# One planned order for every engine's queue is replaced by another: attention and a gated FFT convolution on one core

## The chip, the core and the metric

The kernel runs on one NeuronCore of a Trainium2 chip. The metric is the device time of one execution in microseconds (us). Before the change three runs gave 368.68, 367.60 and 368.24 us; their median is 368.24 us.

## What is computed

Eight batches go through attention with 12 heads of width 64 over 448 positions, whose softmax has an extra `exp(-m)` in the denominator. The heads are put side by side into 768 columns, and a gated convolution follows.

```python
scores = scale * np.matmul(q, k.transpose(0, 1, 3, 2))
m = np.max(scores, axis=-1, keepdims=True)
e = np.exp(scores - m)
attn = e / (np.sum(e, axis=-1, keepdims=True) + np.exp(-m) + 1e-09)
x = heads_side_by_side(np.matmul(attn, v))        # 8 x 448 x 768
proj = x @ w_proj                                 # 768 -> 3 * 768
x1, x2, x3 = the three thirds of proj
x2_conv = irfft(rfft(x2) * rfft(filter))          # along the 448 positions
out = (x1 * x2_conv * x3) @ w_out
```

## The kernel before

**Tiling.** Two heads make a pair; a batch `b` has six pairs, and the pairs of all batches are numbered `i` from 0 to 47. For a pair the kernel turns k and q so that the head width lies on the partitions (`T`, on TensorE and back by VectorE, for batches 0 and 1; `kT` and `qT`, by DMA transposes of three pairs at a time, from batch 2 on). Then come the scores `S(i, t)` (line 871, 873). `S(i, 0)` is one matmul of the full 128 rows, since the rests of both heads lie in it. `S(i, 1)` to `S(i, 3)` are *score couples*: two matmuls of 64 rows each, one for either head, which run side by side. ScalarE takes the exponentials (lines 884, 890). The product with v is `ER(i)` (eight small matmuls of 64 rows, line 902) and `V(i, 0)`, `V(i, 1)` (12 matmuls of 128 rows each, line 910). VectorE divides (lines 923 to 925) into `xb`.

From `xb` each batch gets its transposed `xT`: batch 0 on TensorE (`X`), the others by two DMA transposes of three pairs each (`X9` stands below for the one that carries pairs 9 to 11; line 977). The dense part of a batch follows: a fold on VectorE, the projection of x2 (`P` for batches 0 and 1, line 1083; `PS(b, 0)` to `PS(b, 5)` from batch 2 on, line 1105, with a DMA transpose `x2(b, 0)` or `x2(b, 1)` after each three, line 1122), the spectrum `Z` (lines 1154, 1158), the product with the filter's spectrum, the inverse `I` (line 1253), the two gates `G` (line 1206; `G4` is the first part of one whose sum over the six tiles is cut in two), and the output product `O` and `O4` (line 1019).

**Where data come from.** SyncE (SP) issues the loads of k, q and v (written `sk`, `sq`, `sv`, and `rk`, `rv` for the remaining 64 rows of all pairs of a batch), the DMA transposes and the stores, in one queue. GpSimd (POOL) casts the loaded tiles to bf16 (`ck`, `cq`, `cv`, `crk`, `crv`) and issues the loads of the weights in the same queue: `w(0)` for the first gate, `w(1,0)` and `w(1,1)` for the projection of x2, `w(2)` for the second gate (line 849), and `wout`.

**What sets the order.** No queue is written out by hand in the source. The kernel lists 2135 steps by `plan.add(engine, cost, want, emit, need, make, ...)`, then `plan.run` plays them through a small model of the core: at each moment an engine takes its next step if that step's needs are made and its room in PSUM and SBUF is free. A tuple `plan.ORDER` with one number for each step fixes the order within each engine: an engine's steps are sorted by their numbers.

```python
want = self.ORDER[len(self.tasks)] if self.ORDER else want + self.SHIFT.get(part, 0.0)
...
cost, dma, run, late = self.TIMES.get(len(self.tasks), (cost, dma, run, late))
...
queue = {e: sorted(t for t in self.tasks if t[2] == e) for e in self.LAT}
...
for i, t in enumerate(queue[e][: 1 if self.ORDER else self.WINDOW]):
```

So with ORDER given the model moves no step within an engine. It still decides which PSUM bank each step gets, and how many dummy matmuls on a zero tile (*fillers*, line 1501) stand on TensorE where the model sees it idle between 4.6 and 44 us (`FILL`, 90% of the idle time at 0.056 us each from 8 us on, `COLD` before). `plan.TIMES` holds the model's numbers for each transfer (issue cost, duration, length of run, lateness), and LANDING, DELAY, EARLY and TURN_ROOM are constants of the same model. The chip itself waits only for the data and the room that a step needs.

Of the kernel before, what the change touches and what calls it, by code (L numbers as in the profile page):

```python
# [1612 lines left out]
```

## Time and profile before

| | |
|---|---|
| runs shown | 367.60, 368.24, 368.68 us (median 368.24) |
| profiled execution, first to last instruction (its span) | 365.4 us |
| TensorE busy | 358.2 us, 98% of the span |
| VectorE, ScalarE, GpSimd busy | 261.7, 263.4, 114.0 us |
| DMA packets | 135299, 69.20 MB |
| granted TensorE clock | 1.000 |

No time of its own is shown for the profiled execution beyond its span; the median of the runs lies 2.84 us above that span, which is what lies around it (launch and end). In the profile PE is TensorE's matmuls and PEld its weight loads; a timeline row gives the start, the length, the engine, the line, the operation, what is written and read, and how many alike follow one another. Matmuls overlap in the pipe, so the length of one (0.35 us) says less than the distance from one start to the next.

### The profile page before, as it was taken

The numbers are of one execution on the slowest core, as the hardware profiler recorded it, in microseconds if no ns is written. First come the engines' busy times: TensorE is split into PE (matmuls) and PEld (weight loads), VectorE is DVE, ScalarE is ACT, GpSimd is POOL, SyncE is SP. The second block draws the span as 40 slices with busy tenths as digits, with TensorE's granted clock in tenths as the row PEclk, the third lists the DMA queues.
The fourth block names the chain that finished last, engine by engine and source line by source line (L and its number), as shares of the span: only waits on it lengthen the run. The fifth ranks groups of instructions, "written<-read, shape, count | busy, mean of one in ns | idle before, by whom it ended". The sixth has DMA issues, their size and how long they took to land. (4 is left out here: it accounts for less than half of the span.)

```text
span 365.4 us, 9379 instructions
## 1 busy us (share of the span) xinstructions
PE 358.2 (98%) x3628; PEld 213.2 (58%) x3629; DVE 261.7 (72%) x671; ACT 263.4 (72%) x453; POOL 114.0 (31%) x247
## 2 busy tenths in 40 slices
PE   7999999999999999999999999999999999999995
PEld 6777665656664555655565555654555556555653
DVE  5669299877899549785777758893677867759570
ACT  6989777778796668875777667888877885465433
POOL 7872363315333454345324442700110000000000
PEclk9999999999999999999999999999999999999999
DMA  8999989999999999999999999999942165035025
GB/s 204 270 253 240 248 170 230 230 207 216 157 251 268 249 225 247 200 268 229 260 215 224 309 206 210 210 226 189 219 108 43 45 88 131 0 88 130 26 110 175
DMA packets 135299, 69.20 MB, mean 189 GB/s; under 512 B 91917, under 2 KB 131664, under 8 KB 135248
## 3 DMA queue, kind: packets, MB, share of 16 engines
q1 hardware_dynamic: 130528, 62.90, 78.4%
q0 software_dynamic: 4480, 5.41, 8.8%
q8 instruction: 29, 0.48, 0.6%
q10 hardware_dynamic: 240, 0.23, 0.2%
q14 instruction: 22, 0.18, 0.2%
HBM read 43.86 MB, written 11.01 MB: 150 GB/s over the span
## 5 line engine op out<-in xcount | busy, mean ns | idle before, releaser
L884 ACT ACTIVATE e<-psum 128x896 bf16<-128x896 f32 x138 | 123.0, 922 | 28.8 <-PE psum L871 23.7
L1206 PE MATMUL psum<-xT,wproj_bf 128*128 128x448 bf16 x576 | 121.7, 352 | 0.2 <-DMA xT<-xb 0.2
L1206 PEld LDWEIGHTS <-wproj_bf 128*128 128x128 bf16 x576 | 53.9, 98 | 46.6 <-issue 3.4
L1019 PE MATMUL psum<-wout_bf,yT 128*128 128x384 bf16 (+2 forms) x287 | 54.1, 326 | 0.2
L1105 PE MATMUL psum<-xf,wproj_bf 128*128 128x456 bf16 x216 | 45.7, 356 | 0.0
L910 PE MATMUL psum<-vn,e 128*128 128x65 bf16 x1104 | 45.1, 194 | 0.0
L910 PEld LDWEIGHTS <-e 128*128 128x128 bf16 x1104 | 39.8, 98 | 8.9 <-issue 4.5
L871 PE MATMUL psum<-qT,kT 64*128 64x448 bf16 x288 | 41.9, 354 | 0.2 <-DMA kT<-nat 0.2
L1172 DVE TENSOR_TENSOR t<-xs,hrs 113x768 bf16<-113x768 bf16 (+1 forms) x64 | 39.1, 631 | 3.0 <-ACT xs L1166 2.8
L1222 DVE TENSOR_TENSOR g<-x,psum 128x448 bf16<-128x448 bf16 x42 | 26.0, 618 | 19.0 <-PE psum L1206 16.2
L1332 ACT COPY osb<-psum 128x384 f32<-128x384 f32 (+2 forms) x56 | 26.0, 485 | 17.7 <-PE psum L1019 13.1
L668 POOL CAST nat<-nat 112x512 bf16<-112x512 f32 x36 | 24.3, 679 | 44.1 <-DMA nat<-in_q_dram 44.1
L1166 ACT CAST xs<-psum 113x384 bf16<-113x384 f32 (+1 forms) x64 | 29.1, 484 | 12.3 <-PE psum L1154 8.4
L1019 PEld LDWEIGHTS <-yT 128*128 128x128 bf16 x288 | 27.1, 98 | 18.5 <-issue 1.2
L925 DVE TENSOR_TENSOR xb<-psum,den 128x512 bf16<-128x512 f32 x48 | 33.2, 691 | 1.7
L1220 ACT CAST x<-psum 128x448 bf16<-128x448 f32 x42 | 22.4, 539 | 13.3 <-PE psum L1206 11.7
L700 POOL CAST vn<-nat 128x192 bf16<-128x192 f32 x58 | 21.7, 406 | 32.9 <-DMA nat<-in_v_dram 31.0
L1262 ACT CAST cr<-psum 128x452 bf16<-128x452 f32 x48 | 24.5, 544 | 10.1 <-PE psum L1253 9.2
L1105 PEld LDWEIGHTS <-wproj_bf 128*128 128x128 bf16 x216 | 20.1, 98 | 19.7 <-issue 2.4
L890 ACT ACTIVATE er<-psum 128x448 bf16<-128x448 f32 x46 | 25.4, 555 | 6.9 <-PE psum L873 6.2
L688 POOL CAST nat<-nat 128x384 bf16<-128x384 f32 x29 | 17.6, 612 | 26.6 <-DMA nat<-in_k_dram 24.7
L923 DVE TENSOR_SCALAR den<-psum 128x8 f32<-128x8 f32 x48 | 7.9, 164 | 23.9 <-PE psum L910 23.3
(138 smaller groups left out, 482.0 us busy)
## 6 DMA issues: line engine op xcount, KB each, us to landing
...
```

The source lines that it names most:

```text
L871: nc.tensor.matmul(sc[:, u, 0:S], kT[b % 2][c, hp, t, :], qT[b % 2][c, hp, :])
L884: nc.scalar.activation(to, of, AF.Exp, scale=SCALE)
L890: nc.scalar.activation(to, of, AF.Exp, scale=SCALE)
L910: nc.tensor.matmul(out_bank(u)[:, n, :], P["e"][1 + t][:, u * S + n * 128 : u * S + n * 128 + 128], vn[b % 2][:, hp, 4 * u + t, :], start= ...
L925: nc.vector.tensor_tensor(W["xb", b][:, hp].rearrange("p n (u d) -> p u n d", u=2), op[:, :, :, 0:DH], rec[:].unsqueeze(3).to_broadcast([1 ...
L1019: nc.tensor.matmul(ops[:n, : c.stop - c.start], y[:, dt, 0:n], wout_bf[:, dt, c], start=(dt == 0), stop=(dt == NDT - 1),)
L1105: nc.tensor.matmul(pps, wproj_bf[:, kt, D + dt * 128 : D + (dt + 1) * 128], W["xf", b][:, kt], start=(kt == 0), stop=(kt == NDT - 1),)
L1166: nc.scalar.copy(L["xs", par, ch][:K, pg % 2, :], L["Z", pg, ch][:K, :DCH])
L1172: nc.vector.tensor_tensor(t[:K], L["xs", par, ch][:K], h, op=ALU.mult)
L1206: nc.tensor.matmul(p[:, :S], wproj_bf[:, kt, 2 * part * D + dt * 128 : 2 * part * D + (dt + 1) * 128], xT()[:, kt, 0:S], start=(kt == 0), ...
L1222: nc.vector.tensor_tensor(g[:, dt, :], L["x1", dt], p[:, :S], op=ALU.mult)
L1332: (nc.vector.tensor_copy if half else nc.scalar.copy)(L["os", st][:n, c.start + lo : c.start + hi], L["O", st, ch][:n, lo:hi])
```

## The change

Only constants and the two tables of the plan are changed. Every step, its operands and its needs stay as they were.

```diff
-    LANDING = 1.738
-    DELAY = (0.917, 3.66)
-    EARLY = ((3.0, -0.67), (13.0, 0.95))
-    TURN_ROOM = 1.05
+    LANDING = 1.23
+    DELAY = (1.42, 2.33)
+    EARLY = ((0.0, 0.0), (0.0, 0.0))
+    TURN_ROOM = 1.2
...
-    plan.ORDER = (3, 0, 1, 124, 1, 2, 0, 0, 1, 2, 3, 4, 2, 4, 18, 0, 1, 5, 0, 7, ...
-    plan.TIMES = {3: (0.64, 0.05, 256.0, 0.0), 15: (0.58, 0.735, 50.0, 0.104), 16: (0.58, 1.17, 50.0, -0.215), ...
+    plan.ORDER = (1, 0, 3, 144, 2, 3, 0, 0, 4, 1, 2, 3, 4, 1, 27, 0, 4, 5, 0, 4, ...
+    plan.TIMES = {3: (0.64, 0.0456, 305.26, 0.2144), 15: (0.52, 0.7518, 83.32, 0), 16: (0.52, 0.6399, 70.62, 0), ...
```

In TIMES the old table has a lateness of its own for each transfer (between -4.3 and 4.6 us); the new one has one duration and one lateness for each kind of transfer (0 for the loads, between -0.32 and 0.21 us for the others).

Sorting each engine's steps by the two ORDER tuples gives the queues. 590 of PE's 712 steps change place, by 3.7 places on average and 33 at most; SP 218 of 246, ACT 378 of 451, DVE 481 of 548, POOL 153 of 178. What the prediction speaks of:

| queue | before | after |
|---|---|---|
| PE, first steps | spin, bps, T0, T(0) of k, T(0) of q, S(0,0), S(0,1), S(0,2), T(1) | spin, T(0) of q, T(0) of k, S(0,1), S(0,2), S(0,3), bps, T0, T(1), S(0,0) |
| ACT, first steps | sq0, zero ks, sine table, sines, exp table, exponentials of pair 0 | sq0, sine table, sines, exp table, zero ks, exponentials of pair 0 |
| SP, first loads | sk0, rk0, sk1, sq1, sq2, sk2, sv0, sq3 | sk0, rv0, sq1, sk1, rk0, sq2, sk3, sk2 |
| POOL around `w(0)` | ..., cq5, cv3, `w(0)`, crk1, crk1, `w(1,0)`, cq6 | ..., cq5, `w(0)`, cv3, crk1, cv4, crk1, ones, cq6, cq7, cv5, ck7, `w(1,0)` |
| POOL around `w(2)` | cv7, ck10, `w(2)`, wout, cq11 | cv7, cv9, cv10, cq11, `w(2)`, ck10, wout |
| PE: place of the first step that reads `w(0)` | 74 | 72 |
| PE: place of the first step that reads `w(2)` | 129 (second gate, tile 1) | 128 (second gate, tile 0) |
| PE: runs of steps of 64 rows in all / from the first step that reads `w(0)` / from the first that reads `w(2)` | 82 / 66 / 58 | 77 / 64 / 56 |
| longest run (steps) | 3 | 4 |
| PE between the last of PS(2,3..5) and the first Z that reads x2(2,1) | 3 G, 4 V, 4 couples, S(21,0), ER, 2 Z, in 2 runs | 3 G, 2 V, 2 couples, S(21,0), ER, 2 Z, in 1 run |
| PE between the last of PS(4,0..2) and the first Z that reads x2(4,0) | 2 PS, 3 V, 3 couples, S(33,0), 2 ER, 2 G | 2 PS, 4 V, 3 couples, S(33,0), S(34,0), 2 ER |
| PE between the last V of batch 4 and the first G of batch 4 | 3 G, 5 I, 2 O, 2 couples, S(31,0), S(30,0) | 4 G, 5 I, O, O4, 2 couples, S(30,0) |
| PE between the last G of batch 7 and the first closing O of it | O4, O4, O4 | O4, O4 |

A run is a stretch of PE steps of 64 rows (score couples and ER) with no step of more rows between.

More of the change, by code (lines that the diff above doesn't have):

```diff
@@ new lines @@
+    plan.TIMES = {3: (0.64, 0.0456, 305.26, 0.2144), 15: (0.52, 0.7518, 83.32, 0), 16: (0.52, 0.6399, 70.62, 0), 18: (0.52, 0.9263, 103.83, 0), 20: (0.52, 0.7518, 83.32, 0), 21: (0.52, 0.6399, 70.62, 0), 32: (0.52, 0.7518, 83.32, 0), 34: (0.52, 0.9263, 103.83, 0), 36: (0.52, 0.7518, 83.32, 0), 41: (0.52, 0.7518, 83.32, 0), 43: (0.52, 0.9263, 103.83, 0), 45: (0.52, 0.7518, 83.32, 0), 50: (0.52, 0.7518, 83.32, 0), 52: (0.52, 0.9263, 103.83, 0), 54: (0.52, 0.7518, 83.32, 0), 59: (0.52, 0.7518, 83.32, 0), 61: (0.52, 0.9263, 103.83, 0), 63: (0.52, 0.7518, 83.32, 0), 68: (0.52, 0.7518, 83.32, 0), 70: (0.52, 0.9263, 103.83, 0), 72: (0.52, 0.7518, 83.32, 0), 77: (0.52, 0.7518, 83.32, 0), 78: (0.52, 0.6399, 70.62, 0), 80: (0.52, 0.9263, 103.83, 0), 82: (0.52, 0.7518, 83.32, 0), 83: (0.52, 0.6399, 70.62, 0), 91: (0.52, 0.7518, 83.32, 0), 93: (0.52, 0.9263, 103.83, 0), 95: (0.52, 0.7518, 83.32, 0), 100: (0.52, 0.7518, 83.32, 0), 102: (0.52, 0.9263, 103.83, 0), 104: (0.52, 0.7518, 83.32, 0), 109: (0.52, 0.7518, 83.32, 0), 111: (0.52, 0.9263, 103.83, 0), 113: (0.52, 0.7518, 83.32, 0), 118: (0.52, 0.7518, 83.32, 0), 120: (0.52, 0.9263, 103.83, 0), 122: (0.52, 0.7518, 83.32, 0), 127: (0.52, 0.7518, 83.32, 0), 129: (0.52, 0.9263, 103.83, 0), 131: (0.52, 0.7518, 83.32, 0), 136: (0.52, 0.6399, 70.62, 0), 137: (0.52, 0.6399, 70.62, 0), 141: (0.52, 0.9263, 103.83, 0), 143: (1.29, 0.9672, 8.99, -0.3239), 144: (0.52, 0.7518, 83.32, 0), 146: (1.29, 0.7211, 18, -0.3239), 147: (0.52, 0.7518, 83.32, 0), 149: (0.52, 0.9263, 103.83, 0), 151: (1.29, 0.9672, 8.99, -0.3239), 152: (0.52, 0.7518, 83.32, 0), 154: (1.29, 0.7211, 18, -0.3239), 155: (0.52, 0.7518, 83.32, 0), 157: (0.52, 0.9263, 103.83, 0), 159: (1.29, 0.9672, 8.99, -0.3239), 160: (0.52, 0.7518, 83.32, 0), 162: (1.29, 0.7211, 18, -0.3239), 163: (0.52, 0.7518, 83.32, 0), 165: (0.52, 0.9263, 103.83, 0), 167: (1.29, 0.9672, 8.99, -0.3239), 168: (0.52, 0.7518, 83.32, 0), 170: (1.29, 0.7211, 18, -0.3239), 171: (0.52, 0.7518, 83.32, 0), 173: (0.52, 0.9263, 103.83, 0), 175: (1.29, 0.9672, 8.99, -0.3239), 176: (0.52, 0.7518, 83.32, 0), 178: (1.29, 0.7211, 18, -0.3239), 179: (0.52, 0.7518, 83.32, 0), 181: (0.52, 0.9263, 103.83, 0), 183: (1.29, 0.9672, 8.99, -0.3239), 184: (0.52, 0.7518, 83.32, 0), 186: (1.29, 0.7211, 18, -0.3239), 187: (0.52, 0.7518, 83.32, 0), 189: (0.52, 0.6399, 70.62, 0), 190: (0.52, 0.6399, 70.62, 0), 194: (0.52, 0.9263, 103.83, 0), 196: (1.53, 1.6028, 18, -0.3239), 197: (0.52, 0.7518, 83.32, 0), 199: (1.53, 1.8351, 18, -0.3239), 200: (0.52, 0.7518, 83.32, 0), 202: (0.52, 0.9263, 103.83, 0), 204: (0.52, 0.7518, 83.32, 0), 206: (0.52, 0.7518, 83.32, 0), 208: (0.52, 0.9263, 103.83, 0), 210: (0.52, 0.7518, 83.32, 0), 212: (0.52, 0.7518, 83.32, 0), 214: (0.52, 0.9263, 103.83, 0), 216: (1.53, 1.6028, 18, -0.3239), 217: (0.52, 0.7518, 83.32, 0), 219: (1.53, 1.8351, 18, -0.3239), 220: (0.52, 0.7518, 83.32, 0), 222: (0.52, 0.9263, 103.83, 0), 224: (0.52, 0.7518, 83.32, 0), 226: (0.52, 0.7518, 83.32, 0), 228: (0.52, 0.9263, 103.83, 0), 230: (0.52, 0.7518, 83.32, 0), 232: (0.52, 0.7518, 83.32, 0), 234: (0.52, 0.6399, 70.62, 0), 235: (0.52, 0.6399, 70.62, 0), 239: (0.52, 0.9263, 103.83, 0), 241: (1.53, 1.6028, 18, -0.3239), 242: (0.52, 0.7518, 83.32, 0), 244: (1.53, 1.8351, 18, -0.3239), 245: (0.52, 0.7518, 83.32, 0), 247: (0.52, 0.9263, 103.83, 0), 249: (0.52, 0.7518, 83.32, 0), 251: (0.52, 0.7518, 83.32, 0), 253: (0.52, 0.9263, 103.83, 0), 255: (0.52, 0.7518, 83.32, 0), 257: (0.52, 0.7518, 83.32, 0), 259: (0.52, 0.9263, 103.83, 0), 261: (1.53, 1.6028, 18, -0.3239), 262: (0.52, 0.7518, 83.32, 0), 264: (1.53, 1.8351, 18, -0.3239), 265: (0.52, 0.7518, 83.32, 0), 267: (0.52, 0.9263, 103.83, 0), 269: (0.52, 0.7518, 83.32, 0), 271: (0.52, 0.7518, 83.32, 0), 273: (0.52, 0.9263, 103.83, 0), 275: (0.52, 0.7518, 83.32, 0), 277: (0.52, 0.7518, 83.32, 0), 279: (0.52, 0.6399, 70.62, 0), 280: (0.52, 0.6399, 70.62, 0), 284: (0.52, 0.9263, 103.83, 0), 286: (1.53, 1.6028, 18, -0.3239), 287: (0.52, 0.7518, 83.32, 0), 289: (1.53, 1.8351, 18, -0.3239), 290: (0.52, 0.7518, 83.32, 0), 292: (0.52, 0.9263, 103.83, 0), 294: (0.52, 0.7518, 83.32, 0), 296: (0.52, 0.7518, 83.32, 0), 298: (0.52, 0.9263, 103.83, 0), 300: (0.52, 0.7518, 83.32, 0), 302: (0.52, 0.7518, 83.32, 0), 304: (0.52, 0.9263, 103.83, 0), 306: (1.53, 1.6028, 18, -0.3239), 307: (0.52, 0.7518, 83.32, 0), 309: (1.53, 1.8351, 18, -0.3239), 310: (0.52, 0.7518, 83.32, 0), 312: (0.52, 0.9263, 103.83, 0), 314: (0.52, 0.7518, 83.32, 0), 316: (0.52, 0.7518, 83.32, 0), 318: (0.52, 0.9263, 103.83, 0), 320: (0.52, 0.7518, 83.32, 0), 322: (0.52, 0.7518, 83.32, 0), 324: (0.52, 0.6399, 70.62, 0), 325: (0.52, 0.6399, 70.62, 0), 329: (0.52, 0.9263, 103.83, 0), 331: (1.53, 1.6028, 18, -0.3239), 332: (0.52, 0.7518, 83.32, 0), 334: (1.53, 1.8351, 18, -0.3239), 335: (0.52, 0.7518, 83.32, 0), 337: (0.52, 0.9263, 103.83, 0), 339: (0.52, 0.7518, 83.32, 0), 341: (0.52, 0.7518, 83.32, 0), 343: (0.52, 0.9263, 103.83, 0), 345: (0.52, 0.7518, 83.32, 0), 347: (0.52, 0.7518, 83.32, 0), 349: (0.52, 0.9263, 103.83, 0), 351: (1.53, 1.6028, 18, -0.3239), 352: (0.52, 0.7518, 83.32, 0), 354: (1.53, 1.8351, 18, -0.3239), 355: (0.52, 0.7518, 83.32, 0), 357: (0.52, 0.9263, 103.83, 0), 359: (0.52, 0.7518, 83.32, 0), 361: (0.52, 0.7518, 83.32, 0), 363: (0.52, 0.9263, 103.83, 0), 365: (0.52, 0.7518, 83.32, 0), 367: (0.52, 0.7518, 83.32, 0), 369: (0.52, 0.6399, 70.62, 0), 370: (0.52, 0.6399, 70.62, 0), 374: (0.52, 0.9263, 103.83, 0), 376: (1.53, 1.6028, 18, -0.3239), 377: (0.52, 0.7518, 83.32, 0), 379: (1.53, 1.8351, 18, -0.3239), 380: (0.52, 0.7518, 83.32, 0), 382: (0.52, 0.9263, 103.83, 0), 384: (0.52, 0.7518, 83.32, 0), 386: (0.52, 0.7518, 83.32, 0), 388: (0.52, 0.9263, 103.83, 0), 390: (0.52, 0.7518, 83.32, 0), 392: (0.52, 0.7518, 83.32, 0), 394: (0.52, 0.9263, 103.83, 0), 396: (1.53, 1.6028, 18, -0.3239), 397: (0.52, 0.7518, 83.32, 0), 399: (1.53, 1.8351, 18, -0.3239), 400: (0.52, 0.7518, 83.32, 0), 402: (0.52, 0.9263, 103.83, 0), 404: (0.52, 0.7518, 83.32, 0), 406: (0.52, 0.7518, 83.32, 0), 408: (0.52, 0.9263, 103.83, 0), 410: (0.52, 0.7518, 83.32, 0), 412: (0.52, 0.7518, 83.32, 0), 415: (0.82, 2.7174, 96.86, 0.2144), 416: (0.82, 2.7174, 96.86, 0.2144), 417: (1.79, 3.2386, 50.96, 0.2144), 418: (0.82, 5.9973, 375.71, 0.2144), 419: (0.82, 5.9973, 375.71, 0.2144), 420: (0.82, 5.5978, 276.59, 0.2144), 565: (1.53, 1.9221, 18, -0.3239), 603: (1.53, 1.9221, 18, -0.3239), 640: (1.53, 1.9221, 18, -0.3239), 678: (1.53, 1.9221, 18, -0.3239), 715: (1.53, 1.9221, 18, -0.3239), 753: (1.53, 1.9221, 18, -0.3239), 790: (1.53, 1.9221, 18, -0.3239), 828: (1.53, 1.9221, 18, -0.3239), 865: (1.53, 1.9221, 18, -0.3239), 903: (1.53, 1.9221, 18, -0.3239), 940: (1.53, 1.9221, 18, -0.3239), 978: (1.53, 1.9221, 18, -0.3239), 1015: (1.53, 1.9221, 18, -0.3239), 1054: (1.53, 1.9221, 18, -0.3239), 1185: (0.52, 1.11, 50, -0.3024), 1191: (0.52, 1.11, 50, -0.3024), 1196: (0.52, 1.11, 50, -0.3024), 1317: (0.52, 1.11, 50, -0.3024), 1323: (0.52, 1.11, 50, -0.3024), 1328: (0.52, 1.11, 50, -0.3024), 1333: (0.52, 1.4608, 180, -0.3024), 1352: (1.6, 1.8611, 17, -0.3239), 1363: (1.6, 1.8611, 17, -0.3239), 1452: (0.52, 1.11, 50, -0.3024), 1458: (0.52, 1.11, 50, -0.3024), 1463: (0.52, 1.11, 50, -0.3024), 1482: (1.6, 1.8611, 17, -0.3239), 1493: (1.6, 1.8611, 17, -0.3239), 1582: (0.52, 1.11, 50, -0.3024), 1588: (0.52, 1.11, 50, -0.3024), 1593: (0.52, 1.11, 50, -0.3024), 1598: (0.52, 1.4608, 180, -0.3024), 1617: (1.6, 1.8611, 17, -0.3239), 1628: (1.6, 1.8611, 17, -0.3239), 1717: (0.52, 1.11, 50, -0.3024), 1723: (0.52, 1.11, 50, -0.3024), 1728: (0.52, 1.11, 50, -0.3024), 1747: (1.6, 1.8611, 17, -0.3239), 1754: (1.6, 1.8611, 17, -0.3239), 1847: (0.52, 1.11, 50, -0.3024), 1853: (0.52, 1.11, 50, -0.3024), 1858: (0.52, 1.11, 50, -0.3024), 1863: (0.52, 1.4608, 180, -0.3024), 1882: (1.6, 1.8611, 17, -0.3239), 1889: (1.6, 1.8611, 17, -0.3239), 1982: (0.52, 1.11, 50, -0.3024), 1988: (0.52, 1.11, 50, -0.3024), 1993: (0.52, 1.11, 50, -0.3024), 2012: (1.6, 1.8611, 17, -0.3239), 2019: (1.6, 1.8611, 17, -0.3239), 2112: (0.52, 1.4608, 180, -0.3024), 2118: (0.52, 1.11, 50, -0.3024), 2123: (0.52, 1.11, 50, -0.3024), 2126: (0.52, 0.0049, 50, -0.3024), 2130: (0.52, 0.0049, 50, -0.3024)}
```

3 lines of the change are left out of this document (1 added, 2 removed).

## The prediction

> **What bounds the kernel now.** I read the page first, then the busy time by stretches, then the timeline of TensorE, and last the waits.
>
> ```profile
> span 365.4 us, 9379 instructions
> PE 358.2 (98%) x3628; PEld 213.2 (58%) x3629; DVE 261.7 (72%) x671; ACT 263.4 (72%) x453; POOL 114.0 (31%) x247
> ```
>
> ```profile
> 60.70:150.00 89.30, 89.14 (x905) 52.19 (x905) 71.00 (x170) 68.37 (x117) 35.36 (x73) 1.00 1.08 225
> 250.00:349.80 99.80, 99.80 (x880) 56.73 (x878) 67.77 (x183) 65.63 (x121) 3.46 (x8) 1.00 0.43 96
> ```
>
> PE is busy 98% of the span. Of the stretches (length, then busy PE, PEld, DVE, ACT, POOL, clock, DMA share, GB/s) the one from 250 us on has no PE idle at all, and the one from 60.7 to 150 us 0.16 us. An order that does the same work can therefore gain only where PE is busy without need, or where it waits early. The second thing to see is the DMA share: 1.08 between 60.7 and 150 us, 0.43 after 250 us. Until the input is in, the DMA engines are as full as PE.
>
> **Term 1, runs of 64 rows.** How much does a change between steps of 64 and of 128 rows cost? The timeline of PE tells it by the distance between starts.
>
> ```profile
> 351.13 2.43 PE L1206 MATMUL psum<-xT,wproj_bf 128*128 128x448 bf16 x12
> 353.40 0.81 PE L1019 MATMUL psum<-wout_bf,yR 128*128 128x384 bf16 x4
> ...
> 151.90 1.30 PE L1206 MATMUL psum<-xT,wproj_bf 128*128 128x448 bf16 x6
> 153.13 0.74 PE L871 MATMUL psum<-qT,kT 64*128 64x448 bf16 x6
> 153.80 0.36 PE L1206 MATMUL psum<-xT,wproj_bf 128*128 128x448 bf16 x1
> ...
> 73.95 0.55 PE L871 MATMUL psum<-qT,kT 64*128 64x448 bf16 x4
> 74.44 0.82 PE L1019 MATMUL psum<-wout_bf,yT 128*128 128x384 bf16 x4
> ```
>
> Twelve gate matmuls take 353.40 - 351.13 = 2.27 us, 0.189 each, when others of 128 rows follow. Six of them ahead of a score couple take 1.23 us, where 6 x 0.189 = 1.13: entering a run costs 0.10. Three couples take 0.67 us and two take 0.49: 0.18 to 0.19 a couple, and about 0.11 is left over for leaving. A run costs 0.20 us.
>
> The change has 77 runs for 82, but three of those five go before the first step that reads `w(0)`, where PE has time to spare (Term 2). From the first reader of `w(2)` on it is 56 against 58, with one score more (S(11,1) and S(10,3) against S(11,0)): -2 x 0.20 + 0.19 = -0.2 us. It lies on PE, which has no idle there, so it counts in full unless DMA holds PE back (first rival).
>
> The Trainium skill, TensorE: Matmul & The Clock Gate, "What overlaps and what doesn't", says that a weight load overlaps running matmuls only when its row group differs. By that rule equal rows would pay the 98 ns load every time, a run would save it, and this part would be a loss of 0.4 us instead of a gain of 0.4. The trace disagrees: 0.189 us between matmuls of 128 rows has no room for it, so the rule gets no chance of its own.
>
> **Term 2, the start until `w(2)` is read.** The first 35 us are bound by exponentials and by loads.
>
> ```profile
> 7.00 0.23 PE L596 MATMUL psum<-ident_bf,ks 128*128 128x128 bf16 x1 [1.08 <-POOL ks L551]
> 9.19 2.54 ACT L884 ACTIVATE e<-psum 128x896 bf16<-128x896 f32 x3 [2.35 <-PE psum L871]
> L1501 PE MATMUL psum<-idle x101: 217/219/294, 4.7 to 35.0; 128*128 128x128 bf16 x101
> 21.03 0.89 POOL L849 DMA_DIRECT2D wproj_bf<-in_moe_w_proj_dram  x1
> DMA to landing us min/median/max: 13.0/13.0/13.0
> 35.10 2.43 PE L1206 MATMUL psum<-xT,wproj_bf 128*128 128x448 bf16 x12
> 53.03 0.36 PE L873 MATMUL psum<-qT,kT 128*128 128x448 bf16 x1
> 53.48 0.22 PE L562 MATMUL psum<-ident_bf,ks 128*128 128x128 bf16 x1
> ...
> 53.70 0.36 PE L571 MATMUL psum<-ident_bf,ldm 112*128 112x112 bf16 x4
> 54.41 1.14 PE L1083 MATMUL psum<-wproj_bf,xf 128*113 128x384 bf16 x6 [0.35 <-DVE x L1095]
> 60.71 1.50 PE L1206 MATMUL psum<-xT,wproj_bf 128*128 128x448 bf16 x7
> ...
> 45.98 0.51 POOL L523 CAST ldm<-nat 128x384 bf16<-128x384 f32 x1
> 46.43 0.82 POOL L849 DMA_DIRECT2D wproj_bf<-in_moe_w_proj_dram  x1
> DMA to landing us min/median/max: 12.3/12.3/12.3
> ```
>
> ScalarE waits until 9.19 for the first scores, and up to 35.0 PE has time for 101 fillers on the zero tile: it is not the bound there, and steps or runs saved ahead of that point are worth nothing. The new order starts the scores without `rk0`, whose cast PE waits for at 7.00, and takes the copy "zero ks" out of ScalarE's way, so exponentials could start a microsecond or more before 9.19. I count none of that by itself, because the next stop is pinned: `w(0)` is issued at 21.03 and lands 13.0 us later, at 34.0, and the first gate reads it at 35.10. In the new POOL queue `w(0)` still follows cq5 (without cv3, but sq5 is loaded later), so I leave its landing at 34.0. The gate then starts between 34.0 and 35.1; I take 34.6, the middle, since fewer steps stand ahead of it.
>
> From there to the first reader of `w(2)` PE has the same steps as before but for one score: 60.71 - 35.10 = 25.61 us, plus 0.19. In it are two idle stretches: 53.48 - 53.03 less one matmul of 0.19, 0.26, before T(11), and 54.41 - 53.70 less four transposes (0.05 each from the starts 53.48 and 53.70, where four steps take 0.22), 0.5, after it. Ready by PE alone: 34.6 + 25.8 = 60.4 with these stalls, 59.6 without; T(11) now comes five steps or more later among PE's steps, so I take them as gone. `w(2)` itself landed at 46.43 + 12.3 = 58.7; now two casts of v and one of q stand ahead of it in place of one of k (0.51), estimated at 0.8 us more from three casts of about 0.5 against one, less what of them ran before: 59.5. Both ways give the same; I take 59.5 against 60.71, -1.2 us. Ends: 34.0 + 25.8 - 0.8 = 59.0 with `w(2)` no later than now (-1.7), and 61.2 (+0.5), where `w(2)` waits 1.7 longer for sq11, whose load has no row among these, and the stalls stay.
>
> **Term 3, transfers that come in time or late.** The new order puts fewer steps between some transposes and their readers.
>
> ```profile
> PE psum L871 <- DMA kT<-nat: 0.2, 1, 0.2
> ...
> 196.96 1.87 PE L1206 MATMUL psum<-xT,wproj_bf 128*128 128x448 bf16 x9
> 199.00 0.73 PE L1206 MATMUL psum<-xT,wproj_bf 128*128 128x448 bf16 x3 [0.17 <-DMA xT<-xb]
> ...
> 131.91 0.35 PE L873 MATMUL psum<-qT,kT 128*128 128x448 bf16 x1
> 132.10 0.89 PE L910 MATMUL psum<-vn,e 128*128 128x65 bf16 x24
> 132.83 1.29 PE L1206 MATMUL psum<-xT,wproj_bf 128*128 128x448 bf16 x6
> 138.62 0.67 PE L1154 MATMUL psum<-x,ft 113*113 113x384 bf16 x3
> ...
> 132.68 2.73 SPq L1122 DMA_TRANSPOSE x<-xb  x1
> DMA to landing us min/median/max: 5.7/5.7/5.7
> ...
> 210.04 1.43 SPq L1122 DMA_TRANSPOSE x<-xb  x1
> DMA to landing us min/median/max: 5.2/5.2/5.2
> 216.18 0.33 PE L1154 MATMUL psum<-x,ft 113*113 113x384 bf16 x1
> x<-xb SPq DMA_TRANSPOSE x6, 4.8
> ```
>
> x2(2,1) is issued at 132.68, lands at 138.4, and Z reads it at 138.62: 0.2 us to spare. The new order takes two V (132.83 - 132.10 = 0.73), two couples (0.38) and a run (0.20) out of that distance, 1.3 us. x2(4,0) lands at 215.2 for 216.18, 0.9 to spare; two gates go out (12 x 0.189 = 2.27), a V (0.37) and a score (0.19) come in: 1.7 less. If the two take as long as here they are 1.1 and 0.8 late, 1.9 together; if they take the 4.8 of the median, 0.2 and 0.4. I take 0.6, since a transpose issued behind fewer loads should be the quicker one. Against that, the gate that waited for xT at 199.00 (nine matmuls, 1.70, then 0.34 idle) gets one gate in for S(31,0) and part of an O: 1.13 - 0.19 - 0.3 = 0.6 us more (the two products of an O that go, at 0.189 x 384 / 448 = 0.16 each), and its 0.34 goes. The wait for kT stays. Sum +0.3; ends -0.6 (all these waits go) and +2.5.
>
> **The end.** Two O4 instead of three cover the last gate's way through VectorE.
>
> ```profile
> 353.67 0.62 DVE L1222 TENSOR_TENSOR g<-x,psum 128x448 bf16<-128x448 bf16 x1 [0.34 <-PE psum L1206]
> 354.33 0.22 DVE L1297 TENSOR_TENSOR yR<-g,cv 128x128 bf16<-128x128 bf16 x1
> ```
>
> The gate's matmuls end where O4 starts, 353.40; `yR` is there at 354.55, 1.15 later. Two O4 are 8 x 0.16 = 1.3 us of cover: nothing is lost. Moves on ACT, DVE and POOL elsewhere cost nothing while PE's queue covers them: they are busy 72, 72 and 31%.
>
> **Sum.** -0.2 - 1.2 + 0.3 = -1.1 us: a span of 364.3, and 367.1 us with the 2.84 that the median has above the span. That is -0.31%, just past the 0.3% (1.1 us) that a measurement of this kernel can tell from no change. All terms at their good ends give -0.2 - 1.7 - 0.6 = -2.5 (365.7), all at their bad ends +2.8 (371.0).
>
> **Rivals.**
> *DMA pins the middle (no change).* The kT that PE waits for at 150 us comes off queues that are 108% busy from 60.7 us on. Its place among SP's transfers hardly moves, so if the queues never run dry it lands when it did, and PE just waits longer: the 1.2 us of Term 2 is given back, and -0.2 - 0.3 + 0.6 is left, about 0: 368.2 us. For it: that wait, and the small margins above. Against it: the waits for late transfers are 0.2 us each, and SP itself stood waiting often.
> *Late x2 transposes (slower).* Without a lateness fitted for each transfer, the new order trusts one duration by kind. At the two places above and at the similar ones of batches 3 and 5 to 7, PE waits for the transpose. It decides once these take over 6 us instead of 4.8: then 1.2 more at each of the two tight ones, and as much again at one or two others, 3 us in all: 369.9 us. For it: 5.7 us has been seen. Against: after 250 us the DMA share is 0.43, so no more than three batches are exposed.
> *A start that pays more (faster).* If ScalarE's earlier start moves all of batch 0 and `w(0)` comes a microsecond sooner with it, the end is at the good ends of Term 1 and 2 with Term 3 at 0: 368.24 - 0.2 - 1.7 = 366.3 us. Against: `w(0)` hangs on loads, not on ScalarE.
>
> **Chances.** My forecast 0.30 (its own range 366.4 to 367.8, two thirds of it beyond the 0.3%), DMA pins 0.25, late x2 0.22, a better start 0.23. Faster by over 0.3%: the better start, and 0.2 of the forecast, 0.43; within 0.3%: 0.35; slower: 0.22. Range 365.5 to 369.8: just past the good ends together, and nearly the whole of the slow case.
>
> **What would show it.** Runs: entries and exits of 64 rows in PE's timeline still at 0.10 and 0.11 us, five runs fewer. Start: the first gate at 34.6, the first reader of `w(2)` at 59.5; the first exponential before 9.19. Late transfers: rows of PE waiting for x at the Z of batches 2 and 4, none for xT at the gate of batch 4. The prediction is wrong if the first gate comes after 35.1, or if PE's waits for DMA between 60 and 250 us add up to more than 1.5 us.

## The result and the profile after

| | before | after |
|---|---|---|
| median of 20 runs each, us | 367.96 (366.46 to 370.59) | 370.95 (368.35 to 376.21) |
| ratio | | 1.0072, 95% interval 1.0051 to 1.0094 |
| span of the profiled execution, us | 365.4 | 369.3 |

The changed kernel is slower by 0.7%, about 2.7 us; 367.1 was forecast, with a range up to 369.8. Ratios leave out the few runs that lie more than 1.5% above the shortest of their kernel, here that of 376.21 us, whose granted clock was 0.991. The two profiled executions lie 3.9 us apart, because that of the kernel before lies about 0.9 us below its median. The page of the changed kernel:

```profile
span 369.3 us, 9366 instructions
PE 358.0 (97%) x3614; PEld 212.3 (57%) x3614; DVE 257.2 (70%) x671; ACT 261.9 (71%) x452; POOL 110.5 (30%) x247
```

PE is as busy as before (358.0 us against 358.2), and the other engines are busy 1.5 to 4.5 us less: the change added no work. What was added is waiting, and PE's list of waits names it (what PE waited for, us in total, times, longest), first before and then after:

```profile
PE psum L596 <- POOL ks L551: 1.1, 1, 1.1
PE psum L1083 <- DVE x L1095: 0.4, 1, 0.4
...
PE psum L1206 <- DMA xT<-xb: 0.2, 1, 0.2
PE psum L871 <- DMA kT<-nat: 0.2, 1, 0.2
```

```profile
PE psum L910 <- POOL vn L536: 1.1, 1, 1.1
...
PE psum L596 <- DVE bt L796: 0.9, 1, 0.9
PE psum L1019 <- ACT osb L1332: 0.7, 1, 0.7
PE psum L1154 <- DMA x<-xb: 0.6, 2, 0.4
...
PE psum L871 <- DMA kT<-nat: 0.5, 1, 0.5
PE psum L1019 <- DVE yT L1297: 0.3, 1, 0.3
PE psum L1083 <- DMA wproj_bf<-in_moe_w_proj_dram: 0.3, 1, 0.3
```

In the order of the span these are the start (L596, L910, L1083), the middle (L1019 for yT, L1154, L871) and the end (L1019 for osb). The start, in PE's timeline and POOL's:

```profile
26.00 0.55 PE L871 MATMUL psum<-qT,kT 64*128 64x448 bf16 x2
27.70 0.89 PE L910 MATMUL psum<-vn,e 128*128 128x65 bf16 x24 [1.15 <-POOL vn L536]
...
36.14 1.11 PE L1206 MATMUL psum<-xT,wproj_bf 128*128 128x448 bf16 x5
...
61.63 1.68 PE L1206 MATMUL psum<-xT,wproj_bf 128*128 128x448 bf16 x8
```

```profile
20.16 0.89 POOL L849 DMA_DIRECT2D wproj_bf<-in_moe_w_proj_dram  x1
21.05 0.64 POOL L536 CAST vn<-nat 128x192 bf16<-128x192 f32 x2
26.13 0.51 POOL L551 CAST ks<-rests 64x384 bf16<-64x384 f32 x1 [4.44 <-DMA rests<-in_k_dram]
26.70 1.24 POOL L536 CAST vn<-nat 128x192 bf16<-128x192 f32 x2
27.89 0.50 POOL L551 CAST ks<-rests 64x384 bf16<-64x384 f32 x1
...
31.64 0.83 POOL L849 DMA_DIRECT2D wproj_bf<-in_moe_w_proj_dram  x1
```

POOL's queue stood for 4.44 us at the cast `crk1`, because the load `rk1` (from place 18 to 21 on SP) landed at 25.98 us instead of 20.43. Behind it stood `cv4`, for which PE's V waits 1.15 us, and `w(1,0)`, issued at 31.64 instead of 23.16. `w(0)` itself was issued earlier than before (20.16 against 21.03) and landed at 32.6: it did not set the first gate, which starts at 36.14 instead of 35.10.

The end, by the rows of the branch (line 1561; name of the queue, operation, length in ns, first and last start), before and then after:

```profile
L1561 SPq COMPARE_BRANCH  x1: 58/58/58, 352.7 to 352.7; - x1
L1561 SPq EVENT_SEMAPHORE  x8: 17/17/17, 355.3 to 355.9; - x8
```

```profile
L1561 ACTq COMPARE_BRANCH  x1: 50/50/50, 355.5 to 355.5; - x1
L1561 SPq COMPARE_BRANCH  x1: 58/58/58, 356.7 to 356.7; - x1
L1561 SPq EVENT_SEMAPHORE  x8: 17/17/17, 360.0 to 360.5; - x8
```

```profile
355.77 0.50 ACT L1332 COPY osb<-psum 128x384 f32<-128x384 f32 x1
360.46 2.18 ACT L1332 COPY osb<-psum 128x384 f32<-128x384 f32 x5 [4.20 <-SPq L1561]
```

```profile
359.14 1.14 PE L1019 MATMUL psum<-wout_bf,yT 128*128 128x384 bf16 x6 [0.20 <-PEq L1561]
360.99 4.06 PE L1019 MATMUL psum<-wout_bf,yT 128*128 128x384 bf16 x24 [0.72 <-ACT osb L1332]
```

The program tests a flag once, at line 1561, and every engine passes that branch. `O(6,1,1)` went from PE's place 681 to 697, its copy on ACT is at 355.77, so SP's last store ahead of the branch, now `store(6,1)`, is issued at 356.29 instead of 350.67, and SP reaches the branch 4.0 us later. From there SP needs 3.3 us more until it signals (360.0), ACT's copies start at 360.46, and PE waits 0.72 us for room. The Trainium skill, Runtime: NRT & Kernel Launch, "Instruction fetch mechanics", says that a taken branch whose target isn't in the fetched window waits for a fetch; the trace agrees with such a gap (2.6 us on SP before, 3.3 after) but does not show what fills it.

**A ruler.** At some of PE's places both orders have exactly the same steps behind them. The time of the first matmul at such a place shows where a kernel loses (us, from the profiles; the experiments are told below):

| PE's place | before | after | h2_startonly | f2_middle | g1_mid | g3_all_sk4 |
|---|---|---|---|---|---|---|
| 134 | 64.13 | 65.44 | 65.79 | 63.86 | 64.05 | 62.98 |
| 282 | 136.04 | 137.99 | 137.83 | 136.55 | 136.03 | 134.50 |
| 482 | 235.36 | 237.71 | 236.59 | 236.16 | 235.38 | 233.86 |
| 701 (first closing O4) | 353.40 | 355.85 | 354.63 | 354.20 | 353.42 | 351.90 |
| 711 (last O) | 360.97 | 364.24 | 362.19 | 361.76 | 360.87 | 359.36 |
| span | 365.4 | 369.3 | 366.6 | 366.1 | 365.3 | 363.8 |

After against before: +1.3 us at 134, +2.4 or so from 482 to 701, +3.9 at the end. A profile is one execution, and the start varies between them: three kernels with the changed start as it is (the changed kernel, e1_tail, h3_tail) reach 134 at 65.2 to 67.1, six with the start of before at 63.9 to 64.9. The profiles of e2_rk1 and g3_all_sk4 below are of the shortest of their twelve runs, that of f4_start_rk1 of its longest.

### The profile page after: what moved, and what is told of

It is laid out like the page before. It is cut to its first block, busy times and chain, and to the rows that moved or that the text cites. A ratio compares the mean times of both kernels' runs of the same rounds, so it can differ in the third digit from the quotient of the medians.

```text
span 369.3 us, 9366 instructions
## 1 busy us (share of the span) xinstructions
PE 358.0 (97%) x3614; PEld 212.3 (57%) x3614; DVE 257.2 (70%) x671; ACT 261.9 (71%) x452; POOL 110.5 (30%) x247
## 5 line engine op out<-in xcount | busy, mean ns | idle before, releaser
L884 ACT ACTIVATE e<-psum 128x896 bf16<-128x896 f32 x138 | 121.6, 921 | 27.7 <-PE psum L871 24.1
L1206 PEld LDWEIGHTS <-wproj_bf 128*128 128x128 bf16 x576 | 54.6, 98 | 48.1 <-issue 3.3
L1019 PE MATMUL psum<-wout_bf,yT 128*128 128x384 bf16 (+2 forms) x288 | 53.9, 326 | 1.2 <-ACT osb L1332 0.7
L910 PE MATMUL psum<-vn,e 128*128 128x65 bf16 x1104 | 43.7, 194 | 1.1 <-POOL vn L536 1.1
L910 PEld LDWEIGHTS <-e 128*128 128x128 bf16 x1104 | 38.9, 98 | 8.9 <-issue 5.7
L871 PE MATMUL psum<-qT,kT 64*128 64x448 bf16 x288 | 41.9, 354 | 0.8 <-DMA kT<-nat 0.5
L668 POOL CAST nat<-nat 112x512 bf16<-112x512 f32 x36 | 22.9, 644 | 56.4 <-DMA nat<-in_q_dram 54.8
L1172 DVE TENSOR_TENSOR t<-xs,hrs 113x768 bf16<-113x768 bf16 (+1 forms) x64 | 35.1, 576 | 6.5 <-ACT xs L1166 6.4
L1019 PEld LDWEIGHTS <-yT 128*128 128x128 bf16 x288 | 26.8, 98 | 19.7 <-issue 2.7
L1105 PEld LDWEIGHTS <-wproj_bf 128*128 128x128 bf16 x216 | 20.3, 98 | 19.0 <-issue 1.5
L688 POOL CAST nat<-nat 128x384 bf16<-128x384 f32 x29 | 16.3, 566 | 34.2 <-DMA nat<-in_k_dram 30.8
```

What stands on the lines that cost most here:

```text
L871: nc.tensor.matmul(sc[:, u, 0:S], kT[b % 2][c, hp, t, :], qT[b % 2][c, hp, :])
L884: nc.scalar.activation(to, of, AF.Exp, scale=SCALE)
L910: nc.tensor.matmul(out_bank(u)[:, n, :], P["e"][1 + t][:, u * S + n * 128 : u * S + n * 128 + 128], vn[b % 2][:, hp, 4 * u + t, :], start= ...
L1019: nc.tensor.matmul(ops[:n, : c.stop - c.start], y[:, dt, 0:n], wout_bf[:, dt, c], start=(dt == 0), stop=(dt == NDT - 1),)
L1105: nc.tensor.matmul(pps, wproj_bf[:, kt, D + dt * 128 : D + (dt + 1) * 128], W["xf", b][:, kt], start=(kt == 0), stop=(kt == NDT - 1),)
L1172: nc.vector.tensor_tensor(t[:K], L["xs", par, ch][:K], h, op=ALU.mult)
```

## The experiments

All ratios are against the kernel before, run on the same chip in the same session, with 95% intervals; the changed kernel stands at 1.0072.

**The end.** e1_tail moves one output step and its copy back.

```diff
 PE:  O4(6,1,0), O(6,2,1), O(6,2,0), O4(6,0,1), O(6,0,1), I, O(6,0,0), O(6,1,0),
+     O(6,1,1),
      I, G, I, G, I, I, G, I,
-     O(6,1,1),
      G, G, G, O4, ...      (ACT's copy of O(6,1,1) moves likewise)
```

> The changed kernel with one output step brought forward again: O(6,1,1) directly behind O(6,1,0) on PE, its copy directly behind the other copy of that tile on ACT; nothing else moved. Theory 1 (the late copy delays store(6,1), SP therefore reaches the branch at 356.7 instead of 352.7, and ACT's first copy behind the branch waits for SP until 360.46): SP is at the branch before 354, ACT's copies start by 358.5, PE's 0.72 us for osb goes, the span falls by 0.9 to 1.4 us, to about 368.1; against the kernel before 1.004. Theory 2 (ACT waits for its own way through the branch, 3 to 4 us from where it arrives, and it arrives at 355.5 because of the copies of x1, which stay): the gain is under 0.5 us. Rival 3 (the end is set by the start and by late transfers alone): no change, 1.007.

1.0072 (1.0035 to 1.0109): no gain. SP is at the branch at 348.9 and PE's wait for osb is gone, as theory 1 has it, but ACT's copies start only at 359.60, not by 358.5:

```profile
357.49 0.82 PE L1019 MATMUL psum<-wout_bf,yR 128*128 128x384 bf16 x4 [0.32 <-DVE yR L1297]
...
359.57 5.04 PE L1019 MATMUL psum<-wout_bf,yT 128*128 128x384 bf16 x29 [0.28 <-PEq L1561]
```

```profile
359.60 1.63 ACT L1332 COPY osb<-psum 128x384 f32<-128x384 f32 x4 [3.86 <-PEq L1561]
```

Now PE waits for yR (the moved step had covered VectorE's way to it), and PE is itself the last at the branch. Places 701 to 711 take 8.19 us, against 8.39 after and 7.56 before. One step is not the tail; the whole tail is, in both directions:

```diff
# h3_tail: changed kernel, from PE's place 676 the steps of batches 6 and 7 in the old order
-PE:  ..., O(6,1,1), G, G, G, O4, O4, O, O, O4, O, | branch | ...
+PE:  ..., O(6,2,0), G, I, G, G, O4, O4, O4, O, O, O, | branch | ...
# with their copies, gates and products (ACT, DVE) and store(6,0), (6,1), (6,2) on SP
# h4_tailonly: the kernel before with the changed tail
```

> The changed kernel with the steps of the tail in the order of the kernel before: from place 676 of PE the steps I, G, O of the last two batches (28 places), the copies, gates and products that belong to them on ACT and DVE, and the last three stores of batch 6 on SP. Theory: what one moved output step alone did not give back (its gain was eaten by a new wait of 0.3 us for yR and one of 0.5 behind the branch) comes back when the last three O4 stand together as before: the distance from the last G to the end is 12.0 us as in the kernel before instead of 13.5, 1.3 to 1.5 us less, 1.0035 against the kernel before. Rival (DVE is late at the end for another reason, since its queue ahead of the last gates is full in the changed order): under 0.5 us, 1.006.

> The kernel before with the steps of the tail in the changed order (the reverse of the third kernel). Theory: the end alone costs 1.0 to 1.5 us, 1.003 to 1.004 against the kernel before, ACT's copies behind the branch released by SP and not by PE. Rival (the tail costs only together with the changed order ahead of it): 1.000 to 1.001.

h3_tail: 1.0013 (0.9989 to 1.0037), a larger gain than was expected. h4_tailonly: 1.0037 (1.0014 to 1.0059), as expected. ACT's first copies behind the branch, first of h3_tail, then of h4_tailonly:

```profile
360.26 1.63 ACT L1332 COPY osb<-psum 128x384 f32<-128x384 f32 x4 [3.61 <-PEq L1561]
```

```profile
358.76 2.18 ACT L1332 COPY osb<-psum 128x384 f32<-128x384 f32 x5 [4.18 <-SPq L1561]
```

Released by PE with the old tail, by SP with the new one, and places 701 to 711 take 7.56 and 8.48 us, whatever the order ahead of them. From 711 to the end it is 4.3 and 4.9 us. The tail costs 1.4 us, theory 1 as first told (the late store) plus what the late step had covered.

**The start.** Four kernels move one load or cast, or splice.

```diff
# e2_rk1, on SP
+rk1
 sq5, sq7, sv4
-rk1
# e3_cv4, on POOL
+cv4
 crk1
-cv4
# e4_both: e1_tail and e2_rk1 together
# h2_startonly: changed order up to PE 134, DVE 90, ACT 77, POOL 51, SP 44; then the order before
```

> The changed kernel with the load rk1 moved forward by three places in SP's queue, ahead of the loads sq5, sq7 and sv4 (place 18, as in the kernel before). Theory 1 (POOL stands at the cast crk1 until rk1 lands at 25.98, and cv4, cv5, ck7 and w(1,0) stand behind it): rk1 lands near 21, PE's wait of 1.1 us for cv4 at 25.9 us falls to under 0.5, the first gate starts at 35.0 to 35.4 instead of 36.14, w(1,0) is issued before 28 instead of at 31.64, and the first reader of w(2) is reached 0.8 to 1.4 us earlier, all of which reaches the end: span 368.0 to 368.6, 1.004 against the kernel before. Rival 2 (the loads as a whole are late, since w(0) shares the queues with them from 20.16 on; whichever stands last is late): sv4 or sv5 takes the place of rk1, the first gate stays within 0.3 us of 36.14, no change. Rival 3 (the start gains, but late transfers in the middle take it back): the first reader of w(2) is earlier by 0.8 or more and the span by less than 0.4.

> The changed kernel with the cast cv4 ahead of the first cast of crk1 in POOL's queue instead of behind it; rk1 lands when it did. Theory 1 (head of line): cv4 is cast when sv4 lands, at 22.0 to 22.7, PE's wait of 1.1 us for it goes, but T(6), which needs crk1, waits as long as it did, cv5 and w(1,0) stand where they stood: first gate 0.3 to 1.0 us earlier (35.2 to 35.8), w(1,0) still issued after 31; gain 0.2 to 0.8 us. Rival 2 (rk1 itself is needed at that point by T(6), six steps on): the wait moves from cv4 to T(6) with nearly its whole length, first gate within 0.2 us of 36.14, no gain.

> The edits of the first two kernels together (O(6,1,1) brought forward, rk1 three places forward). Theory 1 for both: the two gains add up, 1.8 to 2.6 us off 369.3, so a span of 366.7 to 367.5, 1.000 to 1.003 against the kernel before; what is left above it is the late transfers between 77 and 220 us (1.5 us more than before). If the start's gain is taken back in the middle, it is the first kernel's time within 0.4 us.

> The reverse splice: the changed order up to the same places, the kernel before from there on. Theory: only the start's cost is in it: 1.3 us, 1.0035 against the kernel before, PE's place 134 at 65 to 66 and then an unchanged distance to the end. Rival (the middle is pinned by transfers that keep their own time): the delay is swallowed by waits that get shorter, 1.000 to 1.001.

e2_rk1: 1.0045 (1.0018 to 1.0071). rk1 lands at 19.3, PE's wait for cv4 is gone, the first gate is at 34.06, the first reader of `w(2)` at 59.07 and place 134 at 62.88, 1.25 us *earlier* than in the kernel before. e3_cv4: 1.0058 (1.0029 to 1.0086), first gate at 35.49, where theory 1 has it; a gain in time is not clear of the noise. e4_both: 1.0023 (0.9999 to 1.0048). h2_startonly: 1.0015 (0.9995 to 1.0035), between theory and rival; in its profile the 1.66 us at place 134 are still 1.22 at 711, so the middle swallows little of it.

But most of these 1.66 us are not the changed start's. h2_startonly keeps the old constants, and with them and the changed start the model puts 118 fillers on TensorE, against 101 before and 86 after. The last 26 stand here, where neither the kernel before nor the changed one has any:

```profile
43.55 1.62 PE L1501 MATMUL psum<-idle 128*128 128x128 bf16 x26
45.00 0.22 PE L562 MATMUL psum<-ident_bf,ks 128*128 128x128 bf16 x1
```

They take 1.45 us of PE, behind a first gate at 35.12, and in g3_all_sk4, which has the changed constants, PE goes on at once at this place. So 1.0015 is not the price of the changed start. f4_start_rk1 and g4_start_sk4 below are spliced in the same way and carry the same 26.

In the profiles of e1, e4, f1, h2 and h3 PE also waits 1.0 to 1.8 us at T(4), near 19 us, for the cast `ck4`: sk4's load had moved too, from SP's place 10 to 16. The last kernels below ask which load counts.

**A splice that went wrong** tells the mechanism best.

```diff
# h1_start: order before up to the same places, then the changed one
 SP (old):    ..., sq12, sk13, sk12, sq13 | qT12, ...
 POOL (new):  ... | crk2, crk2, cq13, cq12, ck13, ck12, ...
# f2_middle: the same, with cq12, ck13, ck12, cq13 on POOL, and the old tail
```

> Spliced order: the kernel before up to where both orders have done the same steps (PE's first 134 places, DVE 90, ACT 77, POOL 51, SP 44), the changed order from there on. Theory (three separate costs: start +1.3 us at place 134, the middle about +1.1, the end +1.4): the start's cost goes, PE's place 134 is reached at 64.1 to 64.4 instead of 65.44, and 1.3 us of it reach the end: 1.0035 against the kernel before, profiled span 367.5 to 368.5. Rival (the middle is pinned by transfers, and a start that is sooner only waits longer there): place 134 early, the last G of the span not, 1.006 to 1.007.

> The splice of h1_start again, mended: start of the kernel before, the changed order from there on, but the casts cq12, ck13, ck12, cq13 on POOL in the order in which the kernel before loads them, and the tail of the kernel before. Only the changed middle is left (PE's places 134 to 676). Theory 1 (in h1_start POOL stood 9.67 us at the cast of q13, whose load is the last of four in the old SP order, so that qT12 on SP and all transfers behind it came 8 us late): that stall is gone, and the time is that of the middle alone, 0.999 to 1.001. Rival (the changed middle loses 1 to 1.5 us to late transfers, as the first pair of profiles had it): 1.003 to 1.004. If h1_start's 8 us had another cause: above 1.01.

h1_start: 1.0209 (1.0170 to 1.0247), the slowest of all. Its POOL:

```profile
66.34 1.17 POOL L668 CAST nat<-nat 112x512 bf16<-112x512 f32 x2 [9.67 <-DMA nat<-in_q_dram]
```

POOL stands 9.67 us at cq13, the first cast of the new order, whose load is the last of the old order; the DMA transpose of q12 on SP waits for cq12 behind it (issued at 67.5, against 59.9 in the changed kernel), and all of SP with it. With the casts in the order of the loads that stall is gone. f2_middle: 1.0020 (1.0001 to 1.0039): between the two expectations, so the changed middle does cost something, about 0.7 us. Between 66 and 355 us its PE waits for VectorE alone, and for no transfer:

```profile
PE psum L871 <- DVE xb L925: 0.8, 1, 0.8
PE psum L1019 <- DVE yT L1297: 0.3, 1, 0.3
```

f3_consts takes the other half of the change, the constants and TIMES with the old ORDER (other PSUM banks, eight fillers fewer).

> The other half of the change: the order of the kernel before with the new constants and the new table of transfer times, so that only the choice of PSUM banks and the number of fillers differ. Theory (banks and fillers cost nothing): 0.999 to 1.001. Rival (other banks bring waits for room): a wait of PE for ACT or DVE that the kernel before does not show, 1.002 or more.

0.9995 (0.9974 to 1.0015): nothing with the old order, as theory has it. The middle costs 0.20% and the tail 0.37%, each measured by itself, so 0.15% of the 0.72% is left for the start. No run measures the start's share alone: that h2_startonly comes to the same 0.15% is chance, because of its fillers. With intervals of 0.2% on either side the three shares are rough.

**The middle.** f1_tail_rk1 has the old tail and rk1 forward; then three small moves.

```diff
# g1_mid = f2_middle with (g2_all = f1_tail_rk1 with)
 PE:  ... Z(2,1,0),
-     Z(2,0,1), Z(2,1,1),
      G, S(22,2), S(22,3), ER(21),
+     Z(2,0,1), Z(2,1,1),
 PE:  ... S(33,0),
-     Z(4,0,0),
      G,
+     Z(4,0,0),
 DVE:
-     cw(3,1),
      division of pair 30,
+     cw(3,1),
```

> The changed kernel with both mendings: the tail in the order of the kernel before (as in h3_tail) and rk1 three places forward in SP's queue (as in e2_rk1). Theory (the loss is a start with one load too late, about 1 us, and a tail, 1.4 us; the middle costs next to nothing): first gate at 34.0 to 35.5, last G to last O's first matmul 7.56 us, 0.998 to 1.000 against the kernel before. Rival (the middle's late transfers cost 1 us or more by themselves): 1.002 to 1.004.

> f2_middle (start and tail of the kernel before, changed middle) with three small moves: the two Z that read x2(2,1) behind the next gate, S(22,2), S(22,3) and ER(21); the first Z that reads x2(4,0) behind the next gate; on DVE one product cw of batch 3 behind the division of pair 30 instead of ahead of it. Theory (the middle's 0.2% are these three waits): PE waits there for none of them, places 134 to 701 take 288.5 to 289.5 us instead of 290.34, and the time is 0.999 to 1.001 against the kernel before. Rival (waits elsewhere take their place, the middle stays late): 1.002.

> f1_tail_rk1 (the changed kernel with the old tail and rk1 forward) with the same three moves in the middle. Theory: 0.7 us less than f1_tail_rk1, 0.999 to 1.001 against the kernel before. Rival as above: 1.002.

f1_tail_rk1: 1.0023 (0.9998 to 1.0048), the rival's figure: with tail and rk1 mended the middle is left. By the times alone rk1 added nothing to the mended tail here (h3_tail has 1.0013); a share of this size is within the noise. g1_mid: 0.9994 (0.9968 to 1.0019) and g2_all: 0.9993 (0.9969 to 1.0018), both back at the kernel before, as the theory has it. Two of the three waits, in PE's timeline of f1_tail_rk1 and then of e2_rk1:

```profile
217.34 0.37 PE L1154 MATMUL psum<-x,ft 113*113 113x384 bf16 x1 [1.46 <-DMA x<-xb]
```

```profile
204.08 0.37 PE L871 MATMUL psum<-qT,kT 64*128 64x448 bf16 x2 [1.03 <-DVE xb L925]
```

The second is a score couple that waits for the division of pair 30 to free its bank, and this is VectorE in e2_rk1 just then, and below it POOL:

```profile
199.14 1.77 DVE L1060 TENSOR_TENSOR xf<-w 128x342 bf16<-128x342 bf16 x2
200.84 1.96 DVE L1271 TENSOR_TENSOR cw<-cr 128x452 bf16<-128x452 bf16 x1
...
203.34 0.69 DVE L925 TENSOR_TENSOR xb<-psum,den 128x512 bf16<-128x512 f32 x1 [0.23 <-DVE den L924]
...
208.93 0.40 DVE L1271 TENSOR_TENSOR cw<-cr 128x452 bf16<-128x452 bf16 x1
```

```profile
199.53 0.63 POOL L700 CAST vn<-nat 128x192 bf16<-128x192 f32 x2
200.11 0.60 POOL L688 CAST nat<-nat 128x384 bf16<-128x384 f32 x1
200.67 0.52 POOL L1492 DMA_DIRECT2D first<-in_moe_w_out_dram  x1
201.18 0.52 POOL L688 CAST nat<-ks 128x384 bf16<-128x384 f32 x1
201.63 0.62 POOL L668 CAST nat<-nat 112x512 bf16<-112x512 f32 x1
202.19 0.80 POOL L700 CAST vn<-nat 128x192 bf16<-128x192 f32 x2
```

The product `cw` takes 1.96 us beside that train of POOL instructions, and 0.40 alone. This wait (0.8 to 1.2 us) stands in four of the eight profiles with the changed middle (h1_start aside), not in that of the changed kernel itself; in three of the other four PE had been held up before, waiting for kT. With cw behind the division places 373 to 432 take 30.46 us in all five kernels that have the move, as in the four without the wait, against 31.5 in f2_middle. So it is this move that gives back the middle's loss in g1_mid; f2_middle had no wait for x2 to lose. The move at x2(2,1) was no gain: places 282 to 327 take 21.0 us with it, 20.2 to 20.9 without.

**Which load, and a version that beats both.**

```diff
# g3_all_sk4 = g2_all and g4_start_sk4 = f4_start_rk1 with, on SP
+sk4
 sk6, sv3, sk5
-sk4
# f4_start_rk1: changed start with rk1 forward, then the order before
# k1_sk4_only: g3_all_sk4, but rk1 back at SP's place 21
# k2_no_z2: g3_all_sk4, but the two Z of x2(2,1) where the change had them
```

> The changed order up to PE's place 134 with rk1 three places forward, the kernel before from there on. Theory (the changed start is the better one as soon as rk1 is in time; in e2_rk1's profile PE's place 134 came at 62.88 instead of 64.13): place 134 at 62.9 to 64.3, and 0.3 to 1.2 us of it reach the end: 0.997 to 0.999. Rival (the middle takes the gain back in waits for transfers): 1.000.

> g2_all with the load sk4 three places forward on SP, ahead of sk6, sv3 and sk5. Theory (the second late load of the start: POOL stands at the cast ck4, and T(4) on PE waits 1.0 to 1.8 us for it): that wait is under 0.3 us, the first gate comes at 33.5 to 34.5, place 134 at 62.5 to 63.5, and the time is 0.5 us or more under that of g2_all: 0.997 to 0.999. Rival (w(0) pins the gate): place 54 earlier, the first gate and the time as in g2_all.

> f4_start_rk1 (changed start with rk1 forward, the rest of the kernel before) with sk4 three places forward as well. Theory: the start is 0.5 us or more sooner than in f4_start_rk1, place 134 at 62.5 to 63.5, 0.997 to 0.999 against the kernel before; then it beats both kernels. Rival: as f4_start_rk1, 0.999 to 1.000.

> g3_all_sk4 without the move of rk1: old tail, three moves in the middle, sk4 forward, rk1 where the change put it (place 21). Theory 1 (rk1 is the load that matters: POOL stands at crk1, cv4 and w(1,0) behind it): PE waits again 0.8 us or more at 24 to 29 us, the first gate is at 35 to 36, and the time is 0.5 to 1.2 us above that of g3_all_sk4, 0.999 to 1.000. Theory 2 (sk4 alone was late): as g3_all_sk4, 0.997.

> g3_all_sk4 without holding back the two Z that read x2(2,1); the moves at x2(4,0) and of cw on DVE stay. Theory (holding them back cost 0.8 us at places 282 to 327, more than the wait of 0.1 to 0.5 us that it removed): places 215 to 327 take 54.8 to 55.2 us instead of 55.46, and the time is 0.3 to 0.6 us under that of g3_all_sk4: 0.995 to 0.997. Rival (the wait for x2(2,1) comes back with its full length): 0.997 to 0.998.

| | ratio | 95% interval | median, us | first gate | first reader of w(2) |
|---|---|---|---|---|---|
| f4_start_rk1 | 0.9994 | 0.9972 to 1.0016 | 367.86 | 35.48 | 62.35 |
| g4_start_sk4 | 0.9989 | 0.9963 to 1.0015 | 367.84 | 34.30 | 61.18 |
| g3_all_sk4 | 0.9973 | 0.9947 to 0.9999 | 367.21 | 34.16 | 59.18 |
| k1_sk4_only | 1.0030 | 1.0004 to 1.0056 | 368.88 | 36.09 | 61.10 |
| k2_no_z2 | 0.9993 | 0.9967 to 1.0019 | 367.24 | 34.53 | 59.56 |

f4 and g4 reach place 134 only at 66.15 and 64.98, later than expected; 1.45 us of that is their 26 fillers, which keep them from showing whether the changed start alone beats the old one. With rk1 late again (k1) the first gate goes from 34.16 to 36.09 and PE's wait is back, so theory 1 holds, with more in the time than it said (about 2.1 us):

```profile
PE psum L910 <- POOL vn L536: 1.2, 1, 1.2
```

What sk4 adds is less clear. The first gates of g3 and g4 come 0.8 and 1.2 us before those of g2 and f4, and none of the four kernels with sk4 forward waits for `ck4` at T(4); but g2 did not wait there either. g3_all_sk4, the changed order with five small moves and the old tail, has a span of 363.8 us in its profile and is the only kernel whose interval lies under 1, by a hair; k2, within 0.03 us of it by the median, has no such interval. That the mended order gains 0.2% is likely, not certain. Holding back the two Z made no difference by the median; k2's places 215 to 327 take 55.8 us, not less than 55.46, so its theory failed, and 0.9993 is outside its rival's range too.

## Why the prediction was wrong, point by point

- **Term 1, runs (-0.2): right.** In the changed kernel six gate matmuls take 1.14 us ahead of steps of 128 rows and 1.23 ahead of ER:

```profile
147.74 1.30 PE L1206 MATMUL psum<-xT,wproj_bf 128*128 128x448 bf16 x6
148.88 0.79 PE L1253 MATMUL psum<-bt,yh 113*128 113x113 bf16 x12
...
150.48 1.30 PE L1206 MATMUL psum<-xT,wproj_bf 128*128 128x448 bf16 x6
151.71 0.29 PE L902 MATMUL psum<-vn,er 64*128 64x65 bf16 x8
```

  Taking from all profiles but h1_start's the shortest time of each stretch between places 163 and 482, the new order, with 33 runs there, needs 158.2 us and the old one, with 36, 158.8: 0.2 us a run. The gain is there, below the waits.
- **Term 2, the start (-1.2): the step that failed is "the next stop is pinned", and with it "I leave its landing at 34.0" and "the gate then starts between 34.0 and 35.1".** `w(0)` landed at 32.6, sooner than that, and the gate came at 36.14, later. It was held by casts that the argument never looked at: it followed `w(0)` through POOL's queue, but not the loads that SP had moved back for the casts around it (rk1, sk4), though "crk1" and "cv4" stand in the row of POOL's queue. With both mended the first gate is at 34.16 and 34.53 in g3_all_sk4 and k2_no_z2 (34.6 forecast) and the first reader of `w(2)` at 59.18 and 59.56 (59.5), against 36.14 and 61.63. That is partly luck, because these times were worked out from landings that did not set them: in g3_all_sk4 `w(0)` lands at 32.7, 1.5 us ahead of the gate, and `w(2)` at 58.5, not at 59.5. What was right is the distance from the gate to that reader, 25.61 + 0.19 - 0.8 = 25.0 us; g3_all_sk4 takes 25.02. The first exponential came at 7.46, "before 9.19", as foretold.
- **Term 3, transfers (+0.3): right in kind, and in some of the places.** The changed kernel waits 0.37 us for x2(2,1), whose transfer took 4.9 us, and 0.5 for kT, against 0.2 before; the wait for xT at batch 4's gate went. For x2(4,0) it does not wait; only e1_tail (0.44) and f1_tail_rk1 (1.46) show a wait of 0.15 us or more there. Four of the eight profiles with the changed middle wait 0.37 to 0.58 us for x2(2,1). Not in the term were a longer x2(3,0), 6.1 us (a wait of 0.2), and waits for VectorE: these, and no transfer, stand in f2_middle, which loses 0.7 us.
- **The end, "nothing is lost": the second step that failed, by 1.4 us.** The cover of yR was worked out rightly (no wait for it after), but the moved step ahead of it was not followed to its copy, its store, and SP's way to the branch. The prediction did not mention the branch.
- **The sum.** The 2.84 us put around the span are about 1.75 (371.04 us for the profiled execution after, with a span of 369.3); the other 1.1 is that the profiled execution of before lies that far below the median. That does not move the forecast, which stands on the median.
- **The rivals.** "Late x2 transposes" came nearest in time (369.9), but by the wrong mechanism: all its waits for x are 0.6 us after. "DMA pins the middle" is against h2_startonly, where a late start stays late. "A start that pays more" is what the profiles of e2_rk1 and g3_all_sk4 show at place 134 (62.88 and 62.98 against 64.13), once rk1 is in time. The sign that was named, a first gate after 35.1, did tell it.
